# Filler matmuls ahead of a SwiGLU feed-forward: 18 of 128 stationary columns, or 17 rounds of four of 32 columns side by side

## Chip, core and metric

The kernel runs on one core of a Trainium2 chip. The metric is the time of one execution on the device in microseconds (us). Three runs of the kernel before were timed: 163.31, 163.59 and 163.64 us, with a median of 163.59 us.

## What is computed

```python
B, S, D, F = 1, 2048, 640, 1536          # x: (B, S, D), all bfloat16
g = silu(x @ w_gate)                     # w_gate: (D, F)
u = x @ w_up                             # w_up:   (D, F)
return (g * u) @ w_down                  # w_down: (F, D)
```

## The kernel before

TensorE multiplies a stationary operand (up to 128 x 128, brought in by an LDWEIGHTS instruction) with a moving operand (128 partitions, up to 512 columns) into PSUM. Every matmul of the program is such a pair. The 2048 rows of x are handled in four blocks of 512 (`S_BLK`). For each block and each of 12 slices of 128 columns of the hidden width (`fc`), TensorE accumulates a gate tile `pg` (weights `wg_sb`) and an up tile `pu` (weights `wu_sb`), five matmuls each, since D = 640 is five times 128 (`kd`). ScalarE applies SiLU to `pg` (line 214) and VectorE multiplies by `pu` (line 215) into `aT`. Then the block is multiplied with `wd_sb` into `po_t` (line 261) and `po_a` (line 291) and is stored.

The change lies in `head()`, which prepares the first block. The stationary and the moving side both need x with its columns on the partitions (`xT`). The first 256 rows of x are loaded as they are (`x_sb`, two chunks of 128 rows, one by SyncE's queue, one by ScalarE's), TensorE transposes them into `pt` (line 185, ten matmuls), and ScalarE (`kd` 0 and 1) and VectorE (`kd` 2 to 4) copy them to `xT` (line 190). Rows 256 to 511 arrive by a transposing DMA (`turn_x(HALF, S_BLK)`, line 105). The first four gate slices come in five small loads, one for each `kd` (line 115); the first up slices in two loads (line 83, called at line 121).

`head()` issues on TensorE, in this order (`keep_order` holds it):

- `warm(N_WARM)`: filler matmuls on a tile of ones, whose result `pw` nobody reads. They wait only for the memset of `ones` (line 109) and fill the time in which x is still on its way.
- `transpose_chunk` for the two chunks.
- the gate matmuls of the first four `fc`, in the order of `steps`: eight of 128 moving columns (`kd` 0 of the first 256 rows), 16 of 256 columns (`kd` 1 to 4 of the same rows), then 20 of 256 columns for rows 256 to 511.
- the up matmuls of the four `fc`, each followed by `gate`.

Everything after `head()` is a long stream of full-width matmuls. The queue of SyncE issues its loads in the order of the program; none of them waits for TensorE in the first 9 us.

Of the kernel before, what the change touches and what calls it, by code (L numbers as in the profile page):

```python
# [10 lines left out]
def _body(  # L11
# [8 lines left out]
    nc = tc.nc  # L20
    P = nc.NUM_PARTITIONS
# [16 lines left out]
    HALF = S_BLK // 2  # L38
    DA = 512
    Q = 32  # L40
    N_WARM = 18
    T = 4
    WT_STEP = 4
    ROW_J = 0
# [62 lines left out]
    ones = consts.tile([P, P], bf16)  # L107
# [64 lines left out]
    pw = psum.tile([P, S_BLK], f32, tag="gu", name="pw", bufs=4)  # L172

    def warm(n):
        for _ in range(n):
            nc.tensor.matmul(  # L176
                pw[:, 0:P], lhsT=ones[:], rhs=ones[:], start=True, stop=True
            )

    def transpose_chunk(c, parts):  # L180
        c_sl = slice(c * P, (c + 1) * P)
# [37 lines left out]
    def head():  # L219
        dve, act = nc.vector.tensor_copy, nc.scalar.copy  # L220
        split = [(act, "po_a", 0, 2), (dve, "po_b", 2, KD)]
        pgs = [
            psum.tile([P, S_BLK], f32, tag="gu", name="pg", bufs=4)
            for _ in range(EARLY)
        ]
        warm(N_WARM)
        for c in range(HALF // P):
            transpose_chunk(c, split)

        steps = [(0, 0, P), (0, P, HALF)]  # L230
        steps += [(kd, 0, HALF) for kd in range(1, KD)]
        steps += [(kd, HALF, S_BLK) for kd in range(KD)]
        for kd, c0, c1 in steps:
            for fc in range(EARLY):
                proj_step(pgs[fc], wg_sb, fc, 0, c0, c1, kd)

        for fc in range(EARLY):
            pu = psum.tile([P, S_BLK], f32, tag=("po_a", "po_b")[fc % 2], name="pu")
            proj(pu, wu_sb, fc, 0, 0, S_BLK)
            gate(pgs[fc], pu, 0, fc, S_BLK)  # L240
        keep_order(mybir.EngineType.PE)
        keep_order(mybir.EngineType.Activation)

    head()
    for sb in range(NSB):
# [14 lines left out]
        for kf in range(KF):  # L260
            nc.tensor.matmul(  # L261
                po_t[:],
                lhsT=wd_sb[:, kf, DA:D],
                rhs=aT[:, kf, sb * S_BLK : sb * S_BLK + n_t],
                start=(kf == 0),
                stop=(kf == KF - 1),
# [14 lines left out]
        for j in range(SUB):  # L281
# [6 lines left out]
            for c0, c1, tag in cols:  # L288
                po = psum.tile([P, c1 - c0], f32, tag=tag, name="po_a")
                for kf in range(KF):  # L290
                    nc.tensor.matmul(  # L291
                        po[:],
                        lhsT=aT[:, kf, s0 : s0 + P],
                        rhs=wd_sb[:, kf, c0:c1],
                        start=(kf == 0),
                        stop=(kf == KF - 1),
# [89 lines left out]
def kernel(tc, *args):  # L386
    _body(tc, *args)
    tc.close()
    tc.compile()
    _trim(tc.nc)  # L390
# [30 lines left out]
```

## Time and profile before

| what | value |
|---|---|
| median of three runs | 163.59 us |
| profiled execution: span from first to last instruction | 161.8 us |
| difference of the median and the span | 1.8 us |
| TensorE busy | 159.4 us, 99% of the span, 808 matmuls |
| VectorE / ScalarE busy | 111.0 us (69%) / 42.6 us (26%) |
| fillers (line 176) | 18, mean 313 ns each, first at 0.39 us, last at 2.2 us |
| transposes of `head()` (line 185) | 10, first at 2.31 us |
| first gate matmul (line 193) | 3.71 us |
| first up matmul | 8.79 us |

For the profiled execution the profile gives the span; the time in which it was timed as a whole is not given, so the difference in the third row is taken against the median. In the profile "PE" is TensorE's matmuls and "PEld" its weight loads; "SPq" and "ACTq" are the instructions with which SyncE and ScalarE issue DMAs. The duration of a matmul contains the depth of its pipeline: matmuls that follow each other overlap, so the pace of a stream is the distance from start to start and not the duration. Starts and durations below are in us from the start of the span, unless ns is said.

### The profile page before, as it was taken

The page shows a single profiled execution, that of the slowest core. Times are in us where ns is not written, and L with a number is a line of the kernel's source. Part 1 is how long each engine was busy: PE and PEld are TensorE (multiplying, and loading weights), DVE is VectorE, ACT ScalarE, POOL GpSimd, SP SyncE. Part 2 cuts the span into 40 slices and gives each one's busy share as a digit, 9 for nine tenths or more (in the row PEclk, how much of TensorE's full clock was granted, in tenths as well). Part 3 has the DMA queues.
Part 4 walks back from the last instruction along what each step waited for, and adds up shares of the span by engine and source line. Part 5 has one row for each costly group of instructions (what it writes and reads, how often), then busy time and mean ns, then how long its engine had stood idle before and what let it go on. Part 6 is the DMA issues. An engine that isn't in the chain of part 4 may idle for free.

```text
span 161.8 us, 2142 instructions
## 1 busy us (share of the span) xinstructions
PE 159.4 (99%) x808; PEld 77.6 (48%) x808; DVE 111.0 (69%) x250; ACT 42.6 (26%) x74; POOL 0.6 (0%) x6
## 2 busy tenths in 40 slices
PE   8999999999999999999999999999999999999995
PEld 7854444444444444444444444444444444445454
DVE  2034223599569999989919999979964999993001
ACT  5051222112222222211222322221214222222121
POOL 1000000000000000000000000000000000000000
PEclk9999999999999999999999999999999999999999
DMA  6999999934189999003110000000321000000312
GB/s 212 231 351 349 361 248 231 222 75 91 34 192 159 235 236 184 4 0 34 65 65 0 0 4 2 0 0 3 62 67 34 0 0 0 0 0 4 48 41 73
DMA packets 41961, 15.86 MB, mean 98 GB/s; under 512 B 33504, under 2 KB 41824, under 8 KB 41952
## 3 DMA queue, kind: packets, MB, share of 16 engines
q1 hardware_dynamic: 33584, 14.93, 37.0%
q10 hardware_dynamic: 8368, 0.80, 3.5%
q8 instruction: 6, 0.10, 0.3%
q14 instruction: 3, 0.02, 0.1%
HBM read 6.88 MB, written 2.62 MB: 59 GB/s over the span
## 4 chain that ended last, share of the span: by engine, by line
PE 97%; DMA 2%; SPq 0%; DVE 0%; issue 0%
PE pg L193 32%; PE pu L193 32%; PE po_a L291 26%; PE po_t L261 6%; DMA wg_sb<-in_w_gate_dram 2%; SPq L86 0%; DVE ot_b L302 0%
## 5 line engine op out<-in xcount | busy, mean ns | idle before, releaser
L193 PE MATMUL pg<-xT,wg_sb 128*128 128x512 bf16 (+3 forms) x264 | 59.8, 363 | 0.1
L193 PE MATMUL pu<-xT,wu_sb 128*128 128x512 bf16 (+1 forms) x240 | 59.1, 379 | 0.0
L215 DVE TENSOR_TENSOR aT<-sg,pu 128x512 bf16<-128x512 f32 (+1 forms) x48 | 32.7, 682 | 32.3 <-PE pu L193 32.3
L214 ACT ACTIVATE sg<-pg 128x512 f32<-128x512 f32 (+1 forms) x48 | 28.4, 597 | 71.2 <-PE pg L193 67.4
L291 PE MATMUL po_a<-wd_sb,aT 128*128 128x512 bf16 (+4 forms) x228 | 42.8, 348 | 0.0
L147 DVE SCALAR_TENSOR_TENSOR prod<-wgT,x_row 128x640 f32<-128x640 bf16 x48 | 39.4, 821 | 1.5 <-DMA wgT<-in_w_gate_dram 0.4
L147 DVE SCALAR_TENSOR_TENSOR prod<-wuT,x_row 128x640 f32<-128x640 bf16 x48 | 39.4, 821 | 1.0
L193 PEld LDWEIGHTS <-wg_sb 128*128 128x128 bf16 x264 | 25.9, 100 | 26.8 <-DMA wg_sb<-in_w_gate_dram 0.4
L193 PEld LDWEIGHTS <-wu_sb 128*128 128x128 bf16 x240 | 23.4, 98 | 28.1 <-DMA wu_sb<-in_w_up_dram 0.3
L291 PEld LDWEIGHTS <-aT 128*128 128x128 bf16 x228 | 20.8, 98 | 21.7
L300 ACT CAST ot<-po_a 128x512 bf16<-128x512 f32 (+2 forms) x17 | 9.5, 559 | 31.8 <-PE po_a L291 20.2
L261 PE MATMUL po_t<-aT,wd_sb 128*128 128x512 bf16 (+1 forms) x48 | 10.4, 366 | 0.0
L261 PEld LDWEIGHTS <-wd_sb 128*128 128x128 bf16 x48 | 4.7, 98 | 5.1
L302 DVE CAST ot_b<-po_a 128x96 bf16<-128x96 f32 (+1 forms) x2 | 0.5, 240 | 9.7 <-PE po_a L291 9.6
L270 ACT CAST ot_t<-po_t 128x512 bf16<-128x512 f32 (+1 forms) x4 | 2.2, 559 | 11.6 <-PE po_t L261 11.6
L147 DVE DVE_READ_ACCUMULATOR prod<-wgT,x_row 128x1 f32 x48 | 3.9, 82 | 0.0
L147 DVE DVE_READ_ACCUMULATOR prod<-wuT,x_row 128x1 f32 x48 | 3.9, 82 | 0.0
L272 DVE STREAM_TRANSPOSE ot_q<-ot_t 128x512 bf16<-128x512 bf16 (+1 forms) x4 | 2.7, 676 | 1.7 <-ACT ot_t L270 1.7
L190 DVE COPY xT<-pt 128x384 bf16<-128x384 bf16 x2 | 0.7, 358 | 2.9 <-PE pt L185 2.9
L176 PE MATMUL pw<-ones 128*128 128x128 bf16 x18 | 2.1, 313 | 0.4 <-DVE ones L109 0.4
L176 PEld LDWEIGHTS <-ones 128*128 128x128 bf16 x18 | 1.8, 147 | 0.4 <-DVE ones L109 0.4
L119 ACT ACT_TABLE_LOAD x1 | 1.3, 1283 | 1.0 <-issue 1.0
(13 smaller groups left out, 4.7 us busy)
## 6 DMA issues: line engine op xcount, KB each, us to landing
wd_sb<-in_w_down_dram SPq DMA_DIRECT2D x1, 1920.0 KB, 13.0
out_dram<-ot SPq DMA_DIRECT2D x15, 128.0 KB, 1.7
wg_sb<-in_w_gate_dram SPq DMA_DIRECT2D x2, 640.0 KB, 7.9
wu_sb<-in_w_up_dram SPq DMA_DIRECT2D x2, 640.0 KB, 8.6
wu_sb<-in_w_up_dram SPq DMA_DIRECT2D x2, 320.0 KB, 4.7
x_row<-in_x_dram SPq DMA_DIRECT2D x1, 640.0 KB, 5.1
wg_sb<-in_w_gate_dram SPq DMA_DIRECT2D x4, 128.0 KB, 3.4
out_dram<-ot_q ACTq DMA_DIRECT2D x12, 32.0 KB, 1.9
```

The lines of the kernel that those rows point to most:

```text
L119: nc.scalar.activation(silu_first[:], ones[:, 0:1], ACT.Silu)
L147: nc.vector.scalar_tensor_tensor(out=prod[:], in0=wT[:, fc, :], scalar=1.0, in1=x_row[:, t, :], op0=ALU.mult, op1=ALU.mult, accum_out=acc[ ...
L176: nc.tensor.matmul(pw[:, 0:P], lhsT=ones[:], rhs=ones[:], start=True, stop=True)
L190: copy(out=xT[:, k0:k1, c_sl], in_=pt[:])
L193: nc.tensor.matmul(ps[:, c0:c1], lhsT=w_sb[:, kd, fc * P : (fc + 1) * P], rhs=xT[:, kd, sb * S_BLK + c0 : sb * S_BLK + c1], start=(kd == 0 ...
L214: nc.scalar.activation(sg[:, 0:n_s], pg[:, 0:n_s], ACT.Silu)
L215: nc.vector.tensor_tensor(out=aT[:, fc, s0 : s0 + n_s], in0=sg[:, 0:n_s], in1=pu[:, 0:n_s], op=ALU.mult)
L261: nc.tensor.matmul(po_t[:], lhsT=wd_sb[:, kf, DA:D], rhs=aT[:, kf, sb * S_BLK : sb * S_BLK + n_t], start=(kf == 0), stop=(kf == KF - 1),)
L270: nc.scalar.copy(ot_t[:], po_t[:])
L272: nc.vector.transpose(out=ot_q[:], in_=ot_t[:])
L291: nc.tensor.matmul(po[:], lhsT=aT[:, kf, s0 : s0 + P], rhs=wd_sb[:, kf, c0:c1], start=(kf == 0), stop=(kf == KF - 1),)
L300: nc.scalar.copy(ot[:], po[:])
```

## The change

In `warm`, the one matmul with all 128 columns of `ones` as stationary operand becomes four matmuls. Each takes 32 columns of `ones` as stationary operand, streams the same 128 columns and writes to its own 32 partitions of `pw`: 0 to 31, 32 to 63, 64 to 95, 96 to 127. The number of rounds goes from 18 to 17, so that there are 68 matmuls with their weight loads in place of 18. Nothing else changes.

```diff
-    N_WARM = 18
+    N_WARM = 17
...
     def warm(n):
         for _ in range(n):
-            nc.tensor.matmul(
-                pw[:, 0:P], lhsT=ones[:], rhs=ones[:], start=True, stop=True
-            )
+            for q in range(0, P, Q):
+                nc.tensor.matmul(
+                    pw[q : q + Q, 0:P],
+                    lhsT=ones[:, 0:Q],
+                    rhs=ones[:],
+                    start=True,
+                    stop=True,
+                )
```

## The prediction

> **What bounds the kernel now.** I read the page first, then the chain in order of time, then the timeline of the first 9 us. From the page:
>
> ```profile
> span 161.8 us, 2142 instructions
> ...
> PE 159.4 (99%) x808; PEld 77.6 (48%) x808; DVE 111.0 (69%) x250; ACT 42.6 (26%) x74; POOL 0.6 (0%) x6
> ...
> PE 97%; DMA 2%; SPq 0%; DVE 0%; issue 0%
> ```
>
> TensorE is busy for 99% of the span and holds 97% of the chain. The rest of the chain is one load at the start, as the chain in order of time says (start, length, what):
>
> ```profile
> 0.45 3.21 DMA wg_sb<-in_w_gate_dram
> 3.71 5.21 PE pg L193 x44
> 8.92 4.37 PE pu L193 x20
> 13.29 1.08 PE pg L193 x5
> ```
>
> The fillers are not on the chain: from 0.45 to 3.66 it is the first gate weights that come last. So the change can move the time by what the head of the kernel passes on to the stream behind it, and by nothing else. Five full matmuls take 1.08 us, which is 216 ns for 512 columns, or 0.422 ns a column; I use it for TensorE at its full pace. The timeline of the first 9 us:
>
> ```profile
> 0.39 1.84 PEld L176 LDWEIGHTS <-ones 128*128 128x128 bf16 x18 [0.39 <-DVE ones L109]
> 0.39 2.10 PE L176 MATMUL pw<-ones 128*128 128x128 bf16 x18 [0.39 <-DVE ones L109]
> ...
> 2.31 1.25 PE L185 MATMUL pt<-ident,x_sb 128*128 128x128 bf16 x10
> ...
> 2.33 1.91 SPq L105 DMA_TRANSPOSE xT<-in_x_dram  x1
> 2.74 0.37 ACT L190 COPY xT<-pt 128x256 bf16<-128x256 bf16 x1 [0.22 <-PE pt L185]
> 3.06 0.36 DVE L190 COPY xT<-pt 128x384 bf16<-128x384 bf16 x1 [2.73 <-PE pt L185]
> 3.28 0.37 ACT L190 COPY xT<-pt 128x256 bf16<-128x256 bf16 x1 [0.16 <-PE pt L185]
> 3.60 0.36 DVE L190 COPY xT<-pt 128x384 bf16<-128x384 bf16 x1 [0.17 <-PE pt L185]
> 3.71 4.93 PEld L193 LDWEIGHTS <-wg_sb 128*128 128x128 bf16 x44 [0.41 <-DMA wg_sb<-in_w_gate_dram]
> ...
> 4.29 1.15 SPq L83 DMA_DIRECT2D wu_sb<-in_w_up_dram  x2
> ...
> 8.79 0.11 PEld L193 LDWEIGHTS <-wu_sb 128*128 128x128 bf16 x2 [0.15 <-DMA wu_sb<-in_w_up_dram]
> ```
>
> and one filler's duration, from the answer for the tile pw (min/median/max in ns, first and last start):
>
> ```profile
> L176 PE MATMUL pw<-ones x18: 289/314/314, 0.4 to 2.2; 128*128 128x128 bf16 x18
> ```
>
> The stretch of fillers is 2.10 us long and its last matmul lasts 0.314, so the last one starts at 2.18, and 17 steps from start to start take 1.79 us: 105 ns a step, 0.82 ns a column. That is half the full pace: TensorE starts at half its clock, although the column for the granted clock shows 1.00 from the first microsecond. When it goes over to the full pace can be counted (stretch, its length, busy time and matmuls of TensorE, weight loads, clock, DMA share, GB/s, for line 193 alone):
>
> ```profile
> 3.71:4.95 1.24, 1.24 (x10) 1.13 (x11) 1.00 1.01 265
> 4.95:6.53 1.58, 1.58 (x16) 1.37 (x14) 1.00 0.85 183
> ```
>
> Ten matmuls, eight of 128 and two of 256 columns, fill 3.71 to 4.95: 1536 columns at 0.82 are 1.26 us. Behind it 14 weight loads for 256 columns fill 1.58 us, 113 ns each, where 108 is the full pace and 210 the half. So the clock doubles near 4.95, which is 4.56 us behind the first filler.
>
> Three arrivals stand in the head, each told by its issue and its time to landing:
>
> ```profile
> x_sb<-in_x_dram SPq DMA_DIRECT2D x1, 160.0 KB, 2.3
> ```
> ```profile
> xT<-in_x_dram SPq DMA_TRANSPOSE x1, 4.2
> ```
> ```profile
> wu_sb<-in_w_up_dram SPq DMA_DIRECT2D x1, 320.0 KB, 4.5
> ```
>
> x is issued at 0 and lands at 2.3, where the transposes start. The turned rows 256 to 511 are issued at 2.33 and land at 6.53; the second half of the gate matmuls needs them. The first up weights are issued at 4.29 and land at 8.79, where the up matmuls start. The 24 gate matmuls of the first half end at 4.95 + 14 x 0.108 = 6.46, just ahead of the 6.53; the 20 of the second take 20 x 0.108 = 2.16, to 8.7, just ahead of the 8.79. The head of the kernel is thus in step with its loads at 2.3, 3.66, 6.53 and 8.79. Whatever TensorE does earlier than these is waited away; what it does later is passed on.
>
> **The change part by part.** Removed: 18 matmuls at 105 ns, 1.89 us from 0.39 to 2.28. Added: 17 rounds of four matmuls. No DMA, no wait and no other engine's work is moved, and nobody reads pw; what queues behind the fillers on TensorE is the transposes, and behind those the gate matmuls. The 50 more weight loads and 50 more matmuls cost only through the length T of a round.
>
> T is not in the trace, which has no matmul of 32 stationary columns; it is bounded from both sides. From below: each of the four still streams 128 columns, and at the half pace that is 105 ns for all of them if they truly stream side by side. So 17 rounds take no less than 1.79 us, to 2.18, and a gain from this part is excluded, since x isn't there before 2.3. From above: if the four go one behind the other, T is 4 x 105 = 420 ns. Between them lies the pace at which pairs of load and matmul can be issued at all. The nearest row is the shortest matmul of the kernel, at its end, at full clock (busy us of the group, mean ns of one):
>
> ```profile
> L291 PE MATMUL po_a<-wd_sb,aT 128*128 128x64 bf16 x12 | 0.5, 193 | 0.0
> ```
>
> Twelve pairs span 0.5 us with a last one of 0.193: 11 steps in 0.31 us, 28 ns a pair, which is what their 64 columns need (27). So the issue of a pair costs 28 ns or less, and four of them 112 ns or less. I take T = 112: the streams side by side, with the issue as the bound. The fillers then end at 0.39 + 17 x 0.112 = 2.29, where they ended before. The Trainium skill (TensorE: Matmul & The Clock Gate, Part 3) measured three column tiles side by side at 2.38 times the speed of three in a row; an estimate from it is 0.13 of a matmul for each further tile, so T = 105 x 1.39 = 146 ns, an end at 2.87, and after the cover below no more than 0.1 us on the time.
>
> How much T may grow without a cost: the ten transposes hold the array for ten steps of 105, from 2.31 to 3.36, and then TensorE stands until 3.71, when the gate weights are there. This cover is 0.35 us. The copies leave room too: the one that the first gate matmuls need ends at 3.11, the second of ScalarE at 3.65, for matmuls that start at 3.71 + 4 x 0.105 = 4.13. So T up to (2.28 + 0.35 - 0.39) / 17 = 132 ns costs nothing. Beyond that, a delay of the gate matmuls costs half of itself as long as they begin before 4.95, because what is pushed behind 4.95 runs at twice the pace, and the first 0.1 us of it disappears in the waits at 6.53 and 8.79. To lose 0.33 us (0.2%, about what a measurement of this kernel can tell from no change) takes a delay of some 0.9 us behind the cover, or T near 185 ns.
>
> One cost stands at the seam, where the array goes from quarters to the full width. No row shows such a seam. Below, it is nothing; above, I bound it by one matmul's whole duration, 0.31 us, since all that is in flight has then left. It lies in the same cover: 2.29 + 0.31 = 2.60 is inside 2.63. The Trainium skill (TensorEngine Tiling (Array Packing), Key Properties) states that changing the tiling mode drains TensorE; no run here shows it, and it gives no size.
>
> The sum for the likeliest case is 0: fillers +0.01, hidden; seam up to 0.31, hidden; stream behind it unchanged. Against the profiled execution the span stays 161.8 us; with the 1.8 us by which the median of the runs stands above this span, the time stays 163.6 us.
>
> **The rivals.** *The issue is slower than I take it (slower).* At half clock a pair may cost twice the 28 ns, 56 ns, and T is 224 ns. The fillers end at 0.39 + 3.81 = 4.20. Seven transposes run at the half pace until 4.95, three at the full one, until 5.11. ScalarE's second copy ends 0.71 us behind the start of the seventh transpose now (3.65 against 2.31 + 6 x 0.105 = 2.94), so it then ends at 4.83 + 0.71 = 5.54, and the second four gate matmuls wait for it. From there 4 x 0.054 + 16 x 0.108 = 1.94 give 7.48, and 2.16 more 9.64 in place of 8.79: +0.8 us, 164.4. For it: the row at 28 ns is at full clock. Against it: that row is bound by its own columns, so it gives only an upper limit. It decides from T = 185 ns.
>
> *The four run one after the other, so that the change does not do what it says.* T = 420 ns at half clock, 210 behind 4.95: 10.9 rounds by 4.95, the other 6.1 by 6.24, the seventh transpose at 6.56, the second copy until 7.27, then 1.94 and 2.16, until 11.4: +2.6 us, 166.2. A rule speaks for something like it: the Trainium skill (same page and part) says that weight loads overlap running matmuls only where their row groups of the array differ, and here all use the same 128 rows. The trace disagrees: 18 loads, 1.84 us, lie inside the 2.10 us of fillers on the same rows, at a pace that leaves no time for them.
>
> *The clock doubles later.* If quarter-wide fillers count for nothing in what opens the clock, the 4.56 us start with the transposes at 2.31 and end at 6.87. The 1.92 us from 4.95 on then run at half the pace and lose 0.96, less 0.1 of the waits: +0.9 us, 164.5. For it: a quarter of the columns works in each instruction. Against it: side by side, the same share of the array is at work. By the Trainium skill (same page, Part 1) the clock is judged in fixed stretches of 3.4 us; if the one that ends at 4.95 were missed, the next would end at 8.4, and the loss would be 1.7 us, an estimate that gives 165.3; that the loads arrive in step here says nothing for or against it.
>
> *The clock doubles earlier (faster).* Four instructions for one may count for more. With the clock doubled by 3.71, the first 24 gate matmuls take 8 x 0.054 + 16 x 0.108 = 2.16, to 5.87, against 6.46: 0.6 us early. In this profile the wait for the turned rows at 6.53 takes all of it, and 0.0 to 0.1 is left. Only where those loads land earlier than in this execution would up to 0.6 come out: 163.0. Against it stands a further place where loads are in step, the up weights of the next slices:
>
> ```profile
> 14.06 0.89 PEld L193 LDWEIGHTS <-wu_sb 128*128 128x128 bf16 x5 [0.19 <-DMA wu_sb<-in_w_up_dram]
> ```
>
> **How the numbers follow.** No change (T up to 185, clock as now): 0.42, at 163.6, its own range 163.3 to 163.9. Slower issue: 0.17, at 164.4. Later clock: 0.13, 164.5 to 165.3. One after the other: 0.12, at 166.2. Earlier clock with a gain: 0.16, 163.0 to 163.3. Slower by over 0.2% is 0.17 + 0.13 + 0.12 = 0.42, the same 0.42, faster 0.16. The range is 163.0 to 165.3; it leaves out the case of one after the other and the tails of the clock's two cases, less than 0.2 in all.
>
> **What would show it.** Right: 68 fillers whose starts come in fours within 105 to 132 ns; transposes at 2.31 to 2.65; the first gate matmul still released by its weights at 3.71; the first up matmul at 8.79. The slower issue or the row of four shows as fillers that reach 4.2 or 6.2, with no wait for gate weights and the first up matmul at 9.6 or 11.4. The clock's cases show in the count of line 193 between 3.71 and 6.53: fewer than 24 gate matmuls for the later one, all of them by 5.9 for the earlier. If fillers and the first up matmul stand where they were and the time still differs by over 0.2%, then the argument that only the head matters is wrong.

## The result, and the profile after

The changed kernel takes 164.88 us (median of 20 runs), the kernel before, run beside it, 163.65 us (20 runs). The ratio of the compared runs is 1.0054, with a 95% interval of 1.0032 to 1.0077; one run of the changed kernel, at 166.8 us, was a disturbed one and is left out. So it is slower by half a per cent. The other 19 runs have a mean of 164.54 us, the runs of the kernel before one of 163.66; the medians are further apart because the 19 do not scatter about one value and their median falls into the larger of two groups. Seven lie from 163.37 to 163.94 us, where 19 of the 20 of the kernel before lie (163.11 to 163.98), twelve from 164.77 to 165.47 us, with nothing between. The question is what puts an execution into the upper group.

The profiled execution took 163.81 us, so it belongs to the lower group. From the page of the changed kernel:

```profile
span 162.5 us, 2230 instructions
...
PE 159.4 (98%) x846; PEld 78.0 (48%) x858; DVE 111.1 (68%) x250; ACT 42.6 (26%) x74; POOL 0.6 (0%) x6
```

Its timeline of the first 9 us, the answer for the tile pw, and the time to landing of the turned rows:

```profile
0.39 1.74 PEld L177 LDWEIGHTS <-ones 128*32 128x32 bf16 x68 [0.39 <-DVE ones L109]
0.39 2.00 PE L177 MATMUL pw<-ones 128*32 128x128 bf16 x68 [0.39 <-DVE ones L109]
...
2.33 1.44 SPq L105 DMA_TRANSPOSE xT<-in_x_dram  x1
2.56 0.98 PEld L190 LDWEIGHTS <-x_sb 128*128 128x128 bf16 x10 [0.43 <-DMA x_sb<-in_x_dram]
...
3.60 5.58 PE L198 MATMUL pg<-xT,wg_sb 128*128 128x128 bf16 x41
...
9.48 1.63 PEld L198 LDWEIGHTS <-wu_sb 128*128 128x128 bf16 x9 [0.26 <-DMA wu_sb<-in_w_up_dram]
```
```profile
L177 PE MATMUL pw<-ones x68: 286/311/314, 0.4 to 2.1; 128*32 128x128 bf16 x68
```
```profile
xT<-in_x_dram SPq DMA_TRANSPOSE x1, 4.8
```

The 68 fillers fill 2.00 us and the last lasts 0.31, so 16 steps from round to round take 1.69 us, 106 ns each: four fillers in the time of one. The fillers end by 2.2; the transposes wait for x, which lands at 2.52 in this execution, and start 0.04 later, as they did before (2.27 and 2.31). The gate weights are no longer waited for; the first up matmul stands at 9.48 in place of 8.79. These 0.69 us make up the whole difference of the spans (162.5 and 161.8). The last of what they wait for is the up weights at 9.44 (8.75 before), and ahead of them the turned rows at 7.1 (6.53). They are not the price of the change: this execution took about as long as the median one of the kernel before, and a kernel with few instructions below (e2) has its first up matmul at 10.01.

What the change itself moved is in the part of the page on DMA queues, asked for in stretches. For 5.5 to 7.5 us of the kernel before, then the same stretch of the changed kernel, then 13 to 15.5 us of the kernel before (queue: packets, MB, and the sum of the packets' times as a share of 16 engines, which can exceed 100% where packets overlap):

```profile
q1 hardware_dynamic: 986, 0.39, 75.6%
```
```profile
q1 hardware_dynamic: 1429, 0.52, 112.9%
q8 instruction: 1, 0.02, 3.4%
```
```profile
q1 hardware_dynamic: 850, 0.85, 107.1%
q8 instruction: 1, 0.02, 2.7%
```

The queue q8 brings instructions. Each of its packets has 16 KB and takes 0.9 to 1.8 us in these traces, and the program has six. The first starts at 13.8 us before, when all loads that `head()` waits for are in (the last lands at 9.78), and at 6.1 us in the changed kernel, while the turned rows and the up weights come in. TensorE now has 136 instructions ahead of the transposes (68 pairs) in place of 36, and so reaches sooner the place where the next block is sent for: in the kernel before, the changed one and e1 to e10 below, TensorE had started 165 to 185 instructions 2 us before the first fetch. The Trainium skill (Runtime: NRT & Kernel Launch, Instruction fetch mechanics) states that an engine's instructions are refilled in blocks of 16 KiB, 256 instructions, and that the cost is mostly hidden. The traces agree on the size, and on the step: TensorE has issued some 250 more instructions at each further fetch.

### The profile page after: what moved, and what is told of

It reads as the page before. It is cut to its first block, busy times and chain, and to the rows that moved or that the text cites. A ratio compares the mean times of both kernels' runs of the same rounds, so it can differ in the third digit from the quotient of the medians.

```text
span 162.5 us, 2230 instructions
## 1 busy us (share of the span) xinstructions
PE 159.4 (98%) x846; PEld 78.0 (48%) x858; DVE 111.1 (68%) x250; ACT 42.6 (26%) x74; POOL 0.6 (0%) x6
## 4 chain that ended last, share of the span: by engine, by line
PE 97%; DMA 2%; issue 0%; DVE 0%
PE pg L198 32%; PE pu L198 32%; PE po_a L296 26%; PE po_t L266 6%; DMA x_sb<-in_x_dram 2%; PE pt L190 1%; DVE ot_b L307 0%
## 5 line engine op out<-in xcount | busy, mean ns | idle before, releaser
L198 PEld LDWEIGHTS <-wg_sb 128*128 128x128 bf16 x264 | 26.4, 102 | 26.7
L177 PE MATMUL pw<-ones 128*32 128x128 bf16 x68 | 2.0, 311 | 0.4 <-DVE ones L109 0.4
L177 PEld LDWEIGHTS <-ones 128*32 128x32 bf16 x68 | 1.7, 143 | 0.4 <-DVE ones L109 0.4
```

Source lines behind the costliest of these rows:

```text
L177: nc.tensor.matmul(pw[q : q + Q, 0:P], lhsT=ones[:, 0:Q], rhs=ones[:], start=True, stop=True,)
L198: nc.tensor.matmul(ps[:, c0:c1], lhsT=w_sb[:, kd, fc * P : (fc + 1) * P], rhs=xT[:, kd, sb * S_BLK + c0 : sb * S_BLK + c1], start=(kd == 0 ...
```

## Theories and experiments

Theory *fetch*: the further instructions bring the first fetch among the just-in-time loads of the head, and one DMA engine delivers its sixteenth of a load late. Rivals: *width* (quarter-wide fillers open TensorE's clock later), *seam* or *count* (17 rounds end 0.1 us earlier, and the gap ahead of the transposes delays the clock). Ratios below are to the kernel before, run on the same chip.

**Long fillers: does the width matter for the clock?** Four kernels with 80 rounds, profiled once each.

```diff
-    N_WARM = 17
+    N_WARM = 80      # l1 (in the kernel before): 128 columns; l2: four of 32; l3: one of 32; l4: two of 64
```

> 80 fillers of 128 stationary columns in place of 18: far more than the head needs, to see when TensorE's pace doubles while nothing but fillers runs. Both theories (width: narrow fillers count for less in what opens the clock; seam: they count in full, and it is the gap between the last filler and the first transpose that counts) expect the step from 107 to about 54 ns between 3 and 7 us behind the first filler, as in the kernel before, where it came 4.56 us behind it.

> 80 rounds of four fillers of 32 stationary columns. Width: the pace of 107 ns a round stays until the transposes and the gate matmuls have run for some 3 to 5 us, so all 80 rounds take 8.5 us and the pace doubles only at 11 to 14 us. Seam: the step comes 3 to 7 us behind the first filler, as with full-width fillers.

> 80 fillers of 32 stationary columns, in the first quarter of the array alone. Width: no step within the fillers (8.5 us at 107 ns). Seam: a step 3 to 7 us behind the first. If four narrow ones open the clock and one alone does not, what counts is the share of the array at work, and four side by side count in full.

> 80 rounds of two fillers of 64 stationary columns side by side. Width: somewhere between full-width and quarter-width fillers, if the columns of one instruction count; no step if only full-width ones count. Seam: a step 3 to 7 us behind the first filler.

The stretch of fillers in the timelines, for 128 columns, one of 32, two of 64 and four of 32:

```profile
0.39 6.08 PE L176 MATMUL pw<-ones 128*128 128x128 bf16 x80 [0.39 <-DVE ones L109]
```
```profile
0.39 6.29 PE L177 MATMUL pw<-ones 128*32 128x128 bf16 x80 [0.39 <-DVE ones L109]
```
```profile
0.39 6.04 PE L177 MATMUL pw<-ones 128*64 128x128 bf16 x160 [0.39 <-DVE ones L109]
```
```profile
0.39 4.66 PE L177 MATMUL pw<-ones 128*32 128x128 bf16 x224 [0.39 <-DVE ones L109]
7.71 1.52 PE L177 MATMUL pw<-ones 128*32 128x128 bf16 x96 [2.66 <-issue]
```

80 rounds at the half pace would take 8.5 us. The starts of the fillers go over from 107 to 56 ns a round at 3.5, 3.9, 3.4 and 3.3 us, that is 2.9 to 3.5 us behind the first filler, whatever the width, even with one quarter of the array at work. Width has fallen for fillers that go on. By the Trainium skill (TensorE: Matmul & The Clock Gate, Part 1) a stretch of 3.4 us of activity opens the clock; these traces, one for each kernel, come near it with 2.9 to 3.5. The last row holds something else: after 224 matmuls, 448 instructions, TensorE stands for 2.66 us, and what it waits for is none of the program's work ("issue"). The first fetch of 16 KB starts at 5.33, when it has fallen idle, lasts 0.92, and only 1.5 us behind its end TensorE goes on. That was the first sight of the fetch; the theory was made from it.

**Two by two: few or many instructions, full or quarter width.**

```diff
 e1: N_WARM = 18 in the changed kernel             # many, quarter
 e2: N_WARM = 17 in the kernel before              # few, full
 e5: pw[:, q : q + Q], lhsT=ones[:], rhs=ones[:, 0:Q]              # many, full
 e6: pw[q : q + Q, 0 : c * P], lhsT=ones[:, 0:Q], rhs=wide[:, 0:c, :]
     # wide = ones[:, None, :].to_broadcast([P, 4, P]), five rounds,
     # c = 4 in four of them, 1 in the last; the reshaping of pw is left out here   # few, quarter
```

> 18 rounds of four in place of 17: the fillers end where they ended before the change. Count theory (one filler less opens a gap ahead of the transposes, and the clock doubles one stretch later in more of the executions): back to 163.6. Width theory (quarter-wide fillers open the clock later): still near 164.9. Fetch theory (136 in place of 36 TensorE instructions ahead of the transposes bring the 16 KB fetch of further instructions from 13.8 us to 6.1 us, among the loads of the head, and one of them or TensorE itself is late): still near 164.9, fetch near 6 us.

> 17 full-width fillers: the change of the count alone. Count theory: near 164.9. Width and fetch theory: 163.6, within 0.3, with the first fetch of 16 KB near 13.8 us.

> 17 rounds of four fillers that use all 128 stationary columns and stream 32 columns each: as many instructions as the changed kernel, the same 107 ns a round, the array at its full width. Fetch theory: near 164.9, in two groups some 1.3 us apart, the fetch near 6 us. Width theory: 163.6. Count theory: 164.9 too, so it is told from fetch by the 17 full-width fillers of the same call.

> Five rounds of four quarter-wide fillers, four of them streaming 512 columns and the last 128: the time that 17 rounds take, with 40 instructions ahead of the transposes in place of 136. Fetch theory: 163.6 within 0.3, the fetch near 13.8 us. Width theory: near 164.9.

| kernel | instructions ahead of the transposes | median us | ratio, 95% interval |
|---|---|---|---|
| e2, full width | 34 | 163.83 | 1.0010, 0.9988 to 1.0031 |
| e6, quarter width | 40 | 163.59 | 0.9997, 0.9974 to 1.0020 |
| e5, full width | 136 | 164.69 | 1.0056, 1.0029 to 1.0084 |
| e1, quarter width | 144 | 165.04 | 1.0080, 1.0052 to 1.0108 |

The first fetch starts at 15.4 us in e2 and at 13.6 in e6 (13.8 was expected for both), at 5.9 in e5 and at 5.8 in e1. The number of instructions decides, and the width does nothing: full-width fillers in as many pieces cost what the change costs (1.0056 and 1.0054), and quarter-wide ones in few pieces cost nothing. The count theory falls with e2, where 17 full-width fillers cost nothing that the runs resolve, and with e1, whose fillers end where they ended before and which is the slowest. Eight of the twelve runs of e5 are in the upper group (164.66 to 165.72), and all seven of e1 (164.60 to 165.43).

The traces of e1 and e5 are both of upper-group spans (163.9 and 163.4). Their timelines where the second half of the gate matmuls begins:

```profile
8.72 2.34 PE L198 MATMUL pg<-xT,wg_sb 128*128 128x256 bf16 x20 [2.04 <-DMA xT<-in_x_dram]
```
```profile
8.21 2.34 PE L198 MATMUL pg<-xT,wg_sb 128*128 128x256 bf16 x20 [2.01 <-DMA xT<-in_x_dram]
```

with the turned rows' time from issue (at 2.34 and 2.33) to landing, and the instruction queue between 5.8 and 7.6 us, for e1 and then for e5:

```profile
xT<-in_x_dram SPq DMA_TRANSPOSE x1, 6.3
```
```profile
q8 instruction: 1, 0.02, 6.2%
```
```profile
xT<-in_x_dram SPq DMA_TRANSPOSE x1, 5.8
```
```profile
q8 instruction: 1, 0.02, 4.1%
```

TensorE waits 2.0 us for the turned rows. A load reports in 16 parts. In e1 fifteen have landed by 6.53, as before the change, and the sixteenth lands at 8.68; the fetch starts at 5.82 and lasts 1.79 (6.2% of 16 engines for 1.8 us). In e5 fifteen are there by 6.64 and the sixteenth at 8.17; the fetch starts at 5.92 and lasts 1.18. So the packet ends at 7.61 and the part lands at 8.68 in e1, 7.10 and 8.17 in e5: 1.07 us behind the packet in both, although one packet is 0.6 us longer than the other. That is what a shared engine gives; that packet and part share it is inferred from this and is not recorded. In the six traces whose first fetch starts at 11 us or later (the kernel before, e2, e6, e7, e8, e10) the last part of the turned rows lands within 0.03 us of the one before it. The clock is no part of it: in e1 TensorE already has its full pace from 5.0 on, earlier than in the profiled execution of the change, where it came at 6.4. For line 198 of e1:

```profile
3.70:4.95 1.25, 1.25 (x10) 1.15 (x11) 1.00 1.05 251
4.99:6.41 1.42, 1.42 (x15) 1.27 (x13) 1.00 0.95 208
```

Thirteen weight loads for 256 columns in 1.42 us are 109 ns each, the full pace; that trace is nevertheless 1.4 us longer. Over all traces the pace doubles anywhere between 4.3 us (e5) and 6.4 (the change), with full-width fillers as late as 6.1 (e10) and with quarter-wide ones as early as 4.6 (e9).

**The change again, and the fetch elsewhere.**

```diff
 e9:  the changed kernel
 e8:  for _ in range(2 * n): pw[:, 0 : P // 2], lhsT=ones[:], rhs=ones[:, 0 : P // 2]
 e7:  for c in (4, 4, 4, 4, 2): pw[:, 0 : c * P], lhsT=ones[:], rhs=wide[:, 0:c, :]
 e10: the same for c in (4, 4, 4, 4, 4)            # the reshaping of pw is left out here
```

> The changed kernel again, to have a trace of its slower group of executions. Fetch theory: near 164.9; the 16 KB fetch of instructions starts near 6 us, and where it comes before the turned rows 256 to 511 have landed (6.5 without it), these land 1.5 to 2.2 us later, TensorE waits for them as long, and the span is near 163.6; where it comes behind them, they land by 7.1 and the span is near 162.5. Clock theory: the slower span goes with a pace that doubles at 8 us or later, and the turned rows land by 7.1.

> 36 full-width fillers of 64 moving columns in place of 18 of 128: the same 1.9 us with 72 instructions. The fetch starts some 2 us behind the 170th instruction of TensorE in the kernels before it, so near 10.4 us here, behind the turned rows and the first up weights (8.75), ahead of the up weights of slices 4 to 7 (14.02). Fetch theory: 163.6 to 164.0, since what is hit has up to 0.8 us of room. If each further instruction costs something wherever the fetch falls, 36 of them cost 36/100 of 1.25: 164.1 or more.

> Five full-width fillers, four of 512 moving columns and one of 256: 1.9 us with 10 instructions. The fetch moves from 13.8 to about 16.6 us. Fetch theory: no load that is needed at once is hit, 163.3 to 163.6. Instruction count: 163.3 (26 instructions less at 0.0125 us).

> Five full-width fillers of 512 moving columns: the same 10 instructions, but the fillers end at 2.5 us, where x lands in most traces so far (2.27 to 2.67). Fetch theory: as with the shorter ones, within 0.2. If the gap between fillers and transposes costs by a clock that doubles late, 0.1 to 0.4 faster than those.

| kernel | first fetch, us | turned rows land | first up matmul | span | median us | ratio, 95% interval |
|---|---|---|---|---|---|---|
| before | 13.8 | 6.5 | 8.79 | 161.8 | | 1 |
| the change | 6.1 | 7.1 | 9.48 | 162.5 | 164.88 | 1.0054, 1.0032 to 1.0077 |
| e9, the change again | 6.2 | 7.0 | 9.42 | 162.4 | 164.34 | 1.0038, 1.0019 to 1.0058 |
| e5, 136 instructions | 5.9 | 8.2 | 10.39 | 163.4 | 164.69 | 1.0056, 1.0029 to 1.0084 |
| e1, 144 instructions | 5.8 | 8.7 | 10.90 | 163.9 | 165.04 | 1.0080, 1.0052 to 1.0108 |
| e8, 72 instructions | 11.4 | 7.0 | 9.82 | 162.8 | 163.57 | 1.0000, 0.9986 to 1.0014 |
| e7, 10 instructions | 18.2 | 6.8 | 9.11 | 163.3 | 163.56 | 0.9998, 0.9980 to 1.0016 |
| e10, 10 instructions | 18.1 | 7.2 | 9.39 | 162.4 | 163.54 | 0.9989, 0.9977 to 1.0002 |

e9 shows the two groups again, six runs from 163.73 to 164.08 and six from 164.60 to 165.08, but its profiled execution fell into the lower one, so there is no trace of an upper-group execution of the change itself. In its trace and in that of the change the last part of the turned rows is 0.2 us or less behind the one before it; in e5 and e1 it is 1.5 and 2.2 us behind. The time at which the fetch starts does not sort the four, because the load moves along with it: the fetch starts 0.7 to 0.8 us ahead of the landing of the fifteenth part in each of them. A hint lies in the packets: the load closes with 32 packets of 4 bytes, which have all started by 6.5 us in the trace of the change and in that of e9, while e1 has 31 of them by 7.0 and e5 30. So the fetch may have come in ahead of the closing packet of one part in e1 and e5, and behind it in the other two. What decides this in an execution of the change is not shown. The groups stand some 1.3 us apart, less than the 1.6 and 2.1 by which the spans of e5 and e1 exceed the kernel before: its profiled execution was a quick one, and its loads are often later than there without any fetch near them. In e2, with its fetch at 15.4, the first up matmul stood at 10.01.

e8 says that it is the place and not the number. With 36 more instructions the fetch comes at 11.4 (10.4 was expected), behind the turned rows and the first up weights, and costs nothing; a price for each instruction would have given 1.0027 or more, outside the interval (and so is 1.0019, 36 hundredths of the change's 0.0054). Its late first up matmul has no fetch ahead of it:

```profile
9.82 2.55 PE L193 MATMUL pu<-xT,wu_sb 128*128 128x512 bf16 x11 [0.41 <-DMA wu_sb<-in_w_up_dram]
```

Fifteen parts of these up weights have landed by 8.18 us, the last lands at 9.78. A single late part is therefore no mark of a fetch by itself; what ties the fetch to the time is the table of ratios, and the turned rows, whose last part was late only where the fetch stood beside them.

e7 and e10 put the fetch behind all loads of the first block, which are in by 17.9 us (16.6 was expected for e7's fetch), and gain nothing that the runs resolve, so the fetch at 13.8 us of the kernel before was already free; nothing beats that kernel. The span of e7 holds one wait of 1.0 us for ScalarE's copy, which ends at 39.7 us, long behind the head. e10's fillers were meant to end at 2.5 and to close the gap, and an earlier clock was to be worth 0.1 to 0.4 us if the gap costs; no gain shows. Its transposes start at 2.64, since x landed at 2.60, so whether the gap was closed in its other executions is not known.

## Why the prediction was right in its range and wrong in its reason

The time fell into the range, 163.0 to 165.3, but the case that was called likeliest, no change at 163.6, did not come, and none of the three slower cases is what happened. That the range held the time is luck: its upper part was drawn for a later clock and a slower issue. Of the signs that were named, the pace of the rounds and the start of the transposes came; the first gate matmul was not released by its weights, and the first up matmul was not at 8.79. Point by point:

- *Only the head matters, and what is late there is passed on.* Right: in the change, e1 and e5 the first up matmul is late by 0.69, 2.11 and 1.60 us, and the span is longer by 0.7, 2.1 and 1.6. The wait of e7 at 39 us is the one exception in these traces.
- *A round takes 112 ns, the four side by side.* Right; 106 to 107. The issue was not the bound.
- *The cover of 0.35 us ahead of the gate matmuls takes the fillers' end and the seam.* Not put to the test, and not there: x lands at 2.52, and the transposes run up to the first gate matmul at 3.60, with the weights already in. The cover belonged to the one execution that was profiled before. It was not needed either, since the fillers end earlier than before and the first transpose follows x by 0.04 us. If the seam drains the array, that lies in the wait for x.
- *"No DMA, no wait and no other engine's work is moved", and the 100 more instructions "cost only through the length T of a round".* This is the step that failed. Instructions are data too. The page's part on DMA queues showed "q8 instruction: 6, 0.10" before the change, and asked by stretches it would have told of the first fetch at 13.8 us and of a fetch every 250 instructions. 100 more ahead of it put it at 6 us, next to a load with no room, and in e1 and e5 one part of that load came 2.15 and 1.53 us behind the others. The prediction itself had worked out that the turned rows at 6.53 and the up weights at 8.79 have none.
- *The slower issue, the row of four.* Neither: rounds of 107 ns.
- *The clock doubles later.* By its own sign it did so in the profiled execution: 19 gate matmuls had started by 6.53, not 24. It did not cost what was forecast, because the loads came late as well: the last of the gate matmuls starts at 9.23 and needs 0.11, and the up weights land at 9.44. Nor does it come from the width, since e10 with full-width fillers has 19 by then too, and it does not make the slower group, since e1 and e5 have all 24.
- *1.8 us between span and time.* Mis-sized: the profiled run of the change has 163.81 for 162.5, so 1.3. The profiled execution of the kernel before was some 0.5 us faster than its median, and its loads, read as the kernel's own rhythm, were those of a good execution.

## What to carry to other kernels

An instruction that costs no time on its engine can still cost through the code that has to be fetched: count instructions as well as nanoseconds, and see where the fetches of the instruction queue fall against loads that have no room. Filler or warm-up work should be made of few long instructions; with 512 moving columns ten instructions filled the time that 136 had filled, and cost nothing that the runs resolve. When times come in two groups, one profile shows one group, and a neighbouring kernel that lies wholly in the other group gives its trace.

## What was not expected of the hardware

Four column tiles run fully side by side: 106 ns for a round of four at the half pace and 56 ns at the full one, the time of one matmul of 128 columns; their weight loads use the same rows and hide all the same. Fillers in one quarter of the array open the clock too, 3.5 us behind the first, against 2.9 to 3.1 for those that use more of it (one trace each). And TensorE can run out of instructions: 448 of them in 4.4 us, and then 2.66 us of standstill.
